# Making one of seven block products of a sequence transform once for two position pairs

## The chip, the cores and the metric

The kernel runs on one core of a Trainium2 chip. The metric is the device time of one launch in microseconds, the median of several runs. TensorE is called PE here, VectorE DVE, ScalarE ACT, GpSimd POOL and SyncE SP, as the profile names them; SP, POOL and, at the very end, ACT issue the DMAs.

## The reference

One input x (2048 positions, width 512) goes through two branches, and a gate mixes them:

```python
g = _sigmoid((x * gate_w).sum(-1, keepdims=True))
# branch A, Fourier mixing: hidden transform, then sequence transform, real part
a = x @ Wd_re.T                      # "bsd,ed->bse"
b = x @ Wd_im.T
A = Ws_re @ a - Ws_im @ b            # "ts,bse->bte", Ws is 2048 x 2048
# branch B, gated MLP with width 1792
h = relu(x @ W_gate) * (x @ W_up)
B = h @ W_down
out = g * A + (1 - g) * B
```

All data are float32.

## The kernel before

**Precision.** A float32 factor is split into a high part (a cast to fp32r, by ACT) and a low part (the rest, a subtraction by DVE). A product takes three matmuls: high by low, low by high, high by high (`PARTS`). In the trace `ch`, `cl` are the two parts of a right side c, `lh`, `ll` or `lb` those of a left side.

**Seven products in place of eight.** Every large product is cut into 2 x 2 blocks and made by the Winograd form of Strassen's method: seven block products, numbered 1 to 7, of sums of blocks. Product 1 is A11 B11, product 2 is A12 B21; block 11 of the result is their sum. Sums, splits and the combination of the results are work for DVE, ACT and the DMA queues while PE multiplies.

**Stages, in order of PE.** Gate and up projections (`Block`, results h to `hd` in HBM), the hidden transforms (`SpectralBlock`, results to `ad`), the last of the gate and up blocks, the down projection (`Down`, two rounds; it stores B to `out` and -B to `zd`), and then four rounds of the sequence transform (`Sequence`), two with the cosine matrix (m = 0) and two with the sine matrix (m = 1). The four are (m, p) = (0, 0), (0, 1), (1, 1), (1, 0), where p is a pair of position blocks of 512.

**One Sequence.** The left side is the transformed hidden data: its two block rows are halves of the 512 hidden columns (256, that is two tiles of 128), its two block columns halves of the 2048 positions to sum over (eight tiles each). The right side holds the matrix for the pair: `r11` to `r22`, each read in four quarters `jj` of two tiles. A product is 4 quarters x 2 left tiles x 2 x 3 = 48 matmuls of 512 columns; a round is seven of them, in the order 1, 3, 5, 7, 6, 2, 4 (the last round begins with 3, and makes its last part in halves of 256 columns). For each quarter SP loads four blocks of r, DVE adds blocks for four of the products, ACT and DVE split seven right sides. `lb` holds split left sides that were stored to HBM during Down and are fetched again for the sine rounds.

**Results.** Products gather in pairs of banks of PSUM (eight in all). The cosine rounds add their four result blocks to `zd` by accumulating DMAs on POOL's queue. The sine rounds add `zd` to the result, also by such a DMA, multiply by the gate (`gg`) on DVE, and add to `out` by a third.

**Who sets the order.** All steps are recorded with a key, the matmul count at which they are wanted. `Plan.due` turns keys into due times, and `Plan.order` sorts the steps of DVE and ACT by them and chooses, engine by engine, the next one that can start by its own costs (0.22667 us for a matmul, a work time for each operation, a line for all DMAs). A step of DVE or ACT may be placed 40 matmuls ahead of its key (`AHEAD`). The order so found is written out: engines work strictly in that order, and a waiting instruction holds up those behind it. Buffers are `UNITS` = 51 units of 128 x 1024 floats.

The low part of a right side is keyed 24 matmuls ahead of its use and the high part 31 (`LO`, `HI`).

Of the kernel before, what the change touches and what calls it, by code (L numbers as in the profile page):

```python
# [89 lines left out]
class Step:  # L90


    def __init__(self, key, engine, name, a, k):
# [10 lines left out]
        self.after, self.start, self.end, self.due = set(), None, None, None  # L104
# [23 lines left out]

class Plan:
# [5 lines left out]

    ISSUE = {"sync": 0.5, "gpsimd": 0.9, "scalar": 0.5}

# [5 lines left out]
    AHEAD = {"vector": 40, "scalar": 40, "sync": 0, "gpsimd": 0}  # L143

    def __init__(self):
        self.ops, self.bufs, self.now, self.steps, self.key = [], [], 0, [], 0

    def op(self, key, f, *a):
        self.ops.append((key, len(self.ops), f, a))
# [14 lines left out]
    def read(self):  # L164
        self.ops.sort(key=lambda o: o[:2])
        for self.key, _, f, a in self.ops:
            f(*a)
        seen, banks = {}, []
# [17 lines left out]
    def due(self):  # L186

        last, n = {}, self.now
        for s in reversed(self.steps):
# [4 lines left out]
            elif s not in last or s.key > 0:  # L194
                end = self.now - (self.SUMS if "accum_op" in s.k else self.STORES)
                last[s] = min(last.get(s, 1e9), min(s.key + self.REST, max(s.key, end)) * self.MATMUL)
            s.due = last[s] - (s.work + self.LANDING if s.name == "dma_start" else 0)
            for x in s.after:
                last[x] = min(last.get(x, 1e9), s.due - self.WAIT - (x.work if x.name != "dma_start" else 0))

    def order(self):
# [5 lines left out]
        free = dict.fromkeys(todo, 0.0)  # L207
        late, line, live, ends = 0.0, 0.0, 0, []
# [5 lines left out]
        while any(todo.values()):  # L214
# [27 lines left out]
            while ends and ends[0] <= t:  # L242
                ends.pop(0)
                live -= 1
# [14 lines left out]
            for b in {r.base for r in (*s.writes, *s.reads) if r.base.kind == "unit"}:  # L259
                left[b] -= 1  # L260
                if not left[b]:
                    ends.append(max(x.end for x in b.uses))
                    ends.sort()
# [28 lines left out]
def kernel(ctx: ExitStack, tc, xP, xG, wf, wgu, wd, cr, ci, wri, gw, out):  # L292

# [52 lines left out]
    class Pair:  # L346
# [10 lines left out]

        def part(self, n, columns):
            return self.banks[n][:, columns]
# [279 lines left out]
    def gate_row(p, key):  # L639

        b = buf("gg")

        def go():
            load(b.all, gd[2 * KD * p:2 * KD * (p + 1)].rearrange("(j i) p -> j (i p)", j=2).partition_broadcast(P))
        op(key, go)
# [80 lines left out]
    class Left:  # L726


        def __init__(self, source, tiles=(4, 4)):
            self.source, self.tiles = source, tiles  # L730
# [17 lines left out]
        def split(self, m, n, key, step):  # L748
            hi, lo = self.t[m, n] = [buf(f"l{x}{m}", [4, HD], F32R) for x in "hl"]
            raw, s = self.side(m, n), slice(self.tiles[n])  # L750
            if m == 4:
# [7 lines left out]
        def prep(self, n, key, step, to=None):  # L759
# [3 lines left out]
            for m in (1, 5, 7, 6, 2, 3, 4):  # L763
# [13 lines left out]
    SUM = {5: 40, 7: 40, 6: 40, 4: 88}  # L777

    class Round:


        ORDER, last = ORDER_Z, False

        def __init__(self, left, counts):
# [11 lines left out]
            for x in self.ORDER:  # L796
                self.seed(x, plan.now)
                self.products(x)
# [8 lines left out]
        def products(self, x):  # L807
            for jj, n in enumerate(self.counts):
                pe(6 * n, self.product, x, jj)

        def product(self, x, jj, tiles=(0, 1), ps=None, columns=slice(None)):
            c = self.c[x, jj]
            ps = ps or self.ps[{1: "A", 3: "E", 5: "B", 7: "D", 6: "B", 2: "A", 4: "G" if self.last else "D"}[x]]
            first, last = x in (1, 3, 5, 7) and not (self.last and x == 3) and jj == 0, jj == len(self.counts) - 1
            if first:
                ps.new()
            for d in tiles:
                ds = slice(d * P, (d + 1) * P)
                for i in range(self.counts[jj]):
                    j = sum(self.counts[:jj]) + i  # L820
                    l = self.left.t[x, j // 4]
                    for n, (a, b) in enumerate(PARTS):
                        mm(ps.part(d, columns), l[a][:, j % 4, ds], c[b][:, i, columns], start=first and i == 0 and n == 0,
# [6 lines left out]
        def evac(self, x, key):  # L830
# [6 lines left out]
            elif x == 6:  # L837
# [5 lines left out]
                if self.last:  # L843
                    op(key + 18, lambda: E().vector.tensor_sub(self.u2.all, o["22"].all, self.n5.all))
                else:
                    op(key + 34, lambda: E().vector.tensor_sub(self.u2.all, self.w.all, self.n5.all))
            elif x == 2:
                self.middle(key)
            elif x == 4:
                self.end(key)  # L850

        def seed(self, x, key):
            pass

        def middle(self, key):
            op(key, lambda: self.both(E().scalar.copy, self.o["11"], self.ps["A"]))
            self.done("11", key + 6)

        def end(self, key):
            def go():  # L860
                for n in range(2):
                    E().vector.scalar_tensor_tensor(self.o["21"][:, n], self.ps["D"][n], -1.0, self.u2[:, n],
                                                    op0=OP.mult, op1=OP.subtract)
            op(key, go)
            self.done("21", key + 6)
# [23 lines left out]
    HALVES = slice(0, N // 2), slice(N // 2, N)  # L889

    class Half:


        def __init__(self, pair, n):
            self.pair, self.n = pair, n

        def part(self, n, columns):
            return self.pair.part(self.n, columns)


    class Sequence(Round):
        HI, LO = 31, 24

        def __init__(self, left, m, p, last=False):
            self.m, self.p, self.last = m, p, last
            if m:
                self.g = gate_row(p, plan.now + 100)
            if last:
                self.ends = Pair("ze")
                self.half = [Half(self.ends, n) for n in range(2)]  # L910

                self.ORDER = (3, 1, *ORDER_Z[2:])
            super().__init__(left, (2, 2, 2, 2))

        def rights(self):
# [5 lines left out]
            for jj in range(4):  # L921
                r = {b: buf(f"r{b}") for b in BLOCKS}
                for b, key in (("11", at[1, jj]), ("22", at[3, jj]), ("12", at[5, jj]), ("21", at[2, jj] - 36)):
                    op(key - 90, lambda r=r, b=b, jj=jj: load(r[b].all, source(b, jj)))
                for x, (o, i) in {5: ("11", "12"), 7: ("12", "22"), 6: ("11", "22"), 4: ("11", "21")}.items():
                    if self.last and x == 4:

                        op(at[6, jj] - 20, lambda r=r, jj=jj: accumulate(r["11"].all, source("21", jj)))
                        continue
                    op(at[x, jj] - SUM[x], lambda r=r, o=o, i=i: combine(r[o].all, r[o].all, r[i].all, 1))  # L930
                if self.last:
                    g = self.gate("21")
                    op(at[4, jj] - SUM[4] + 2, lambda r=r, g=g: E().vector.scalar_tensor_tensor(
                        r["11"].all, r["11"].all, -1.0, g, op0=OP.mult, op1=OP.mult))
                for x in self.ORDER:
                    self.split(x, jj, r[{1: "11", 3: "22", 5: "11", 7: "12", 6: "11", 2: "21", 4: "11"}[x]])

        def products(self, x):  # L940
            if not self.last or x != 4:
                return super().products(x)
            for jj in range(3):
                pe(6, self.product, x, jj, (1,))
            op(plan.now + 2, self.halve)
            for jj in range(4):
                pe(6, self.product, x, jj, (0,))
            for n, h in enumerate(HALVES):
                pe(3, self.product, x, 3, (1,), self.half[n], h)

        def halve(self):
            self.ends.new()
            for n, h in enumerate(HALVES):
                E().scalar.copy(self.half[n].part(1, h), self.ps["G"].part(1, h))
# [3 lines left out]

        def gate(self, b):
            return self.g[:, int(b[1]) - 1].unsqueeze(1).to_broadcast([P, 2, N])  # L960

        def done(self, b, key):
# [4 lines left out]
            if self.last and b == "12":  # L967
                key += 4
            else:
                op(key, lambda: accumulate(o.all, zd[self.place(b)]))  # L970
                key += 42 if self.last else 62
            op(key, lambda: E().vector.tensor_mul(o.all, o.all, self.gate(b)))
            op(key + 6, lambda: accumulate(out[self.place(b)], o.all))

        def middle(self, key):
            if not self.last:
                return super().middle(key)
            z, v = buf("z"), buf("v")
            op(key - 60, lambda: load(z.all, zd[self.place("11")]))
            op(key - 60, lambda: load(v.all, out[self.place("11")]))  # L980

            def go():
                self.both(E().vector.tensor_add, z, self.ps["A"], z)
                E().vector.tensor_mul(z.all, z.all, self.gate("11"))
# [225 lines left out]
```

## Time and profile before

| | us |
|---|---|
| median of three runs | 795.3 |
| lowest and highest | 794.19, 795.4 |
| the profiled execution | 794.13 |
| its span, first to last instruction | 792.4 |

Times in the tables of the profile are us from the start of the span unless marked ns. A group line reads: line, engine, operation, what is written from what, shapes, count, then busy time, mean ns of one, idle time of the engine ahead of them and what ended it. All lines of the kernel are L126, since one helper issues every instruction; so the names of the tiles tell the groups apart. In the 40 slices a digit is the busy share in tenths.

### The profile page before, as it was taken

How to read it: one execution, taken by the hardware profiler on the slowest of the kernel's cores; microseconds unless marked ns; L12 is line 12 of the kernel's file. 1: busy time of each engine (PE TensorE's matmuls, PEld its weight loads, DVE VectorE, ACT ScalarE, POOL GpSimd, SP SyncE). 2: the span in 40 equal slices, each digit the busy share in tenths (PEclk: the TensorE clock that was granted, in tenths of full speed). 3: DMA queues.
4: the chain of work that ended last, by engine and by line, in shares of the span. 5: the costliest groups of instructions: out<-in, count | busy, mean ns of one | idle time of the engine just before them, and what ended most of it. 6: DMA issues, size and time to landing. Idle time of an engine off the chain costs nothing.

```text
span 792.4 us, 9557 instructions
## 1 busy us (share of the span) xinstructions
PE 787.1 (99%) x3470; PEld 651.5 (82%) x3470; DVE 652.1 (82%) x778; ACT 332.6 (42%) x402; POOL 97.0 (12%) x151
## 2 busy tenths in 40 slices
PE   9999999999999999999999999999999999999997
PEld 7888888888888888888888888888888888888886
DVE  7999986868699466999886799997597549966996
ACT  5533221312133234274665668464343335442631
POOL 0101311111112122111121001001000100011001
PEclk9999999999999999999999999999999999999999
DMA  8614553232548599999899989217877994098766
GB/s 320 250 41 164 180 187 146 93 147 94 199 146 267 194 353 398 416 349 342 296 367 415 411 285 371 87 53 223 259 271 282 282 379 132 31 278 253 199 147 133
DMA packets 53888, 187.02 MB, mean 236 GB/s; under 512 B 6225, under 2 KB 6993, under 8 KB 53841
## 3 DMA queue, kind: packets, MB, share of 16 engines
q1 hardware_dynamic: 33680, 113.40, 39.9%
q0 software_dynamic: 20016, 72.89, 28.1%
q8 instruction: 27, 0.44, 0.2%
q14 instruction: 21, 0.16, 0.1%
q10 hardware_dynamic: 144, 0.13, 0.1%
HBM read 117.18 MB, written 69.21 MB: 235 GB/s over the span
## 4 chain that ended last, share of the span: by engine, by line
PE 99%; ACT 0%; DVE 0%; issue 0%
PE z L126 55%; PE c L126 34%; PE a L126 10%; PE warm L126 0%; PE ze L126 0%; ACT z L126 0%; DVE warm L126 0%
## 5 line engine op out<-in xcount | busy, mean ns | idle before, releaser
L126 ACT CAST ch<-r 128x1024 fp32r<-128x1024 f32 x112 | 116.0, 1052 | 132.4 <-DVE r L126 54.0
L126 PE MATMUL z<-cl,lh 128*128 128x512 f32 x420 | 163.4, 389 | 0.0
L126 PE MATMUL z<-ch,lh 128*128 128x512 f32 x420 | 163.4, 389 | 0.0
L126 PE MATMUL z<-ch,ll 128*128 128x512 f32 x420 | 163.4, 389 | 0.0
L126 DVE TENSOR_TENSOR cl<-r,ch 128x1024 fp32r<-128x1024 f32 x112 | 134.3, 1218 | 30.9 <-ACT ch L126 22.3
L126 PE MATMUL z<-ch,lb 128*128 128x512 f32 x444 | 136.8, 389 | 0.0
L126 PEld LDWEIGHTS z<-ch,lb 128*128 128x128 f32 x444 | 83.3, 188 | 17.3
L126 PEld LDWEIGHTS z<-cl,lh 128*128 128x128 f32 x420 | 78.8, 188 | 16.5
L126 PEld LDWEIGHTS z<-ch,lh 128*128 128x128 f32 x420 | 78.8, 188 | 16.3
L126 PEld LDWEIGHTS z<-ch,ll 128*128 128x128 f32 x420 | 78.8, 188 | 16.2
L126 PE MATMUL z<-cl,lb 128*128 128x512 f32 x222 | 86.4, 389 | 0.0
L126 DVE TENSOR_TENSOR r<-r,r 128x1024 f32<-128x1024 f32 x60 | 71.5, 1216 | 2.8 <-DMA r<-ci 2.5
L126 DVE TENSOR_TENSOR cl<-hr,ch 128x1024 fp32r<-128x1024 f32 (+1 forms) x56 | 59.8, 1085 | 13.2 <-ACT ch L126 11.3
L126 ACT CAST ch<-hr 128x1024 fp32r<-128x1024 f32 (+1 forms) x56 | 51.4, 942 | 27.7 <-DMA hr<-hd 13.2
L126 PEld LDWEIGHTS z<-cl,lb 128*128 128x128 f32 x222 | 41.7, 188 | 8.7
L126 ACT ACTIVATE g<-c 128x512 f32<-128x512 f32 x26 | 15.5, 597 | 62.7 <-PE c L126 62.5
L126 PE MATMUL c<-xl,wb0h 128*128 128x512 f32 x104 | 40.5, 389 | 0.0
L126 PE MATMUL c<-xh,wb0l 128*128 128x512 f32 x104 | 40.5, 389 | 0.0
L126 PE MATMUL c<-xh,wb1h 128*128 128x512 f32 x104 | 40.5, 389 | 0.0
L126 PE MATMUL c<-xh,wb0h 128*128 128x512 f32 x104 | 40.5, 389 | 0.0
L126 PE MATMUL c<-xh,wb1l 128*128 128x512 f32 x104 | 40.5, 389 | 0.0
L126 PE MATMUL c<-xl,wb1h 128*128 128x512 f32 x104 | 40.5, 389 | 0.0
(200 smaller groups left out, 1321.4 us busy)
## 6 DMA issues: line engine op xcount, KB each, us to landing
hr<-hd SPq DMA_DIRECT2D x42, 512.0 KB, 7.1
r<-cr SPq DMA_DIRECT2D x32, 512.0 KB, 4.8
r<-ci SPq DMA_DIRECT2D x32, 512.0 KB, 8.9
hd<-hs POOLq DMA_DIRECT2D x28, 512.0 KB, 4.7
lb<-lb SPq DMA_DIRECT2D x28, 512.0 KB, 4.7
ad<-a POOLq DMA_DIRECT2D x16, 512.0 KB, 6.0
l<-ad SPq DMA_DIRECT2D x16, 512.0 KB, 8.8
wr<-wgu SPq DMA_DIRECT2D x14, 512.0 KB, 6.5
```

The costliest lines, as they stand in the source:

```text
L126: getattr(getattr(nc, self.engine), self.name)(*map(ap, self.a), **{k: ap(x) for k, x in self.k.items()})
```

## The change

Product 2, A12 B21, has the same left side for both position pairs of a matrix. It is taken out of the four `Sequence` rounds, which keep six products (order 1, 7, 6, 3, 5, 4), and is made for both pairs at once in a new class `Joint` after the second and after the fourth round. There A12 (256 x 1024) times the two B21 side by side (1024 x 1024) is again cut into 2 x 2 blocks and made by seven products of 12 matmuls, where two direct products had 48 each. The left sides of a Joint are loaded, summed and split on chip and are not stored to `lb`.

Inside a Sequence the result of product 1 is copied, negated, into the banks in which products 6 and 5 go on (`seed`), so fewer sums are left for DVE; in the sine rounds block 12 of `zd` is copied into the banks of product 3 ahead of it, and block 21 is made ready in SBUF and copied into the banks of product 4. Block 11 is finished after the first product. For product 4, three of the four rounds and both Joints sum the block 21 into r by an accumulating DMA; the round (1, 1) loads it and adds on DVE.

The planner reckons with DMA queues of SP and POOL that send packets in turns, lets SP issue up to 40 matmuls ahead, gives POOL 0.5 us more ahead of a transfer, and takes a landing of 2.1 us, 1.5 us later for sums. The diff, cut to its core:

```diff
 class Step:
-            self.work = n * 4 * P / 4096 * 0.157 / 16 * (2 if "accum_op" in k else 1)
+            self.work = n * 4 * P / 4096 * 0.160 / 16 * (2 if "accum_op" in k else 1)
+class Queues:
+    LANDING, LATER = 2.1, 1.5
+    # add(step, start): packets of the queues that have work go in turns; gives step.end
 class Plan:
+    LATE = {"gpsimd": 0.5}
-    AHEAD = {"vector": 40, "scalar": 40, "sync": 0, "gpsimd": 0}
+    AHEAD = {"vector": 40, "scalar": 40, "sync": 40, "gpsimd": 0}
...
-                line = max(line, free[s.engine]) + s.work
-                s.end = line + self.LANDING + (2.0 if "accum_op" in s.k else 0)
+                queues.add(s, free[s.engine] + self.LATE.get(s.engine, 0))
...
     class Sequence(Round):
+        ORDER, NEW, FOUR = (1, 7, 6, 3, 5, 4), (1, 3, 7), "G"
...
+                r = {b: buf(f"r{b}") for b in ("11", "12", "22")}
+                for b, x, t in (("11", 1, 90), ("12", 7, 110), ("22", 7, 105)):
+                    op(at[x, jj] - t, lambda r=r, b=b, jj=jj: load(r[b].all, source(b, jj)))
+                for x, o, a, b, sign in ((7, "12", "12", "22", 1), (6, "11", "11", "12", 1), (5, "12", "11", "22", -1)):
+                    op(at[x, jj] - 40 if x != 5 else at[6, jj] + 10, ...combine...)
+                if self.fourth:
+                    op(at[6, jj] + 14, lambda r=r, jj=jj: accumulate(r["11"].all, source("21", jj)))
+                else:
+                    ...load r21, combine r11 with it...
...
+            if b in ("11", "22"):
+                op(key, lambda: accumulate(o.all, zd[self.place(b)]))
+                key += 50
+            op(key, lambda: E().vector.tensor_mul(o.all, o.all, g))
+            op(key + 6, lambda: accumulate(out[self.place(b)], o.all))
...
+            if x == 1:
+                op(key, seed)                     # banks B <- -A, by ACT
+                op(key + 1, lambda: both(copy, o["11"], a))
+                self.done("11", key + 6)
+            elif x == 6:
+                op(key, lambda: both(minus, u, b))
+                op(key + 1, lambda: [E().vector.tensor_sub(u[:, n], u[:, n], d[n]) for n in range(2)])
+                if self.m:
+                    op(key + 6, lambda: accumulate(u.all, zd[self.place("21")]))
+                op(key + 50, seed4)               # banks G <- u, by ACT
+            elif x == 5:
+                o["12"] = w
+                op(key, lambda: both(copy, w, b))
+                op(key + 1, lambda: both(E().vector.tensor_add, o["22"], d, w))
+                self.done("22", key + 6)
+                op(key + 7, lambda: both(E().vector.tensor_add, w, e, w))
+                self.done("12", key + 12)
+            elif x == 4:
+                op(key, lambda: both(copy, o["21"], g))
+                self.done("21", key + 6)
+    class Joint:
+        ORDER = (1, 7, 6, 5, 2, 3, 4)
+        def __init__(self, m, last=False):
+            self.m, self.last, self.base, self.lead = m, last, plan.now, 130 if last else 85
...
+            for x in self.ORDER:
+                if last and x == 4:
+                    for h in range(2):
+                        pe(6, self.halves, h)     # bank H0, then H1, 256 columns each
+                else:
+                    for jj in range(2):
+                        pe(6, self.product, x, jj)
+                    self.evac(x, plan.now)
...
+            for x, o, *sums in ((1, "11"), (7, "12", ("12", "12", "22", 1)), (6, "11", ("11", "11", "12", 1)),
+                                (5, "12", ("12", "11", "22", -1)), (2, "21"), (3, "22"), (4, "11")):
+                for a, b, c, sign in sums:
+                    op(at[x] - 6, ...combine...)  # at[x]: place of the product less self.lead
+                if x == 4:
+                    op(at[6] + 6, lambda: accumulate(r["11"].all, source("21")))
...
+            if x == 1:
+                op(key, seed)                     # bank X <- -A, by ACT
+            elif x == 6:
+                op(key, lambda: e.scalar.copy(s, bank("X")))
+                op(key + 1, lambda: e.vector.tensor_add(y, bank("D"), s))
+                if last:
+                    op(key + 2, seed4)            # banks H0, H1 <- v - g y
+            elif x == 5:
+                op(key, lambda: e.vector.tensor_add(o[1][:, 1], bank("B"), y))
+                op(key + 2, done, 1, 1)
...
-        Sequence(lefts[m], m, p, n == 3)
+        Sequence(lefts[m], m, p, n != 2)
+        if n % 2:
+            Joint(m, m == 1)
```

More of the change, by code (lines that the diff above doesn't have):

```diff
@@ L103, in __init__ @@
             self.reads += self.writes
-        self.after, self.start, self.end, self.due = set(), None, None, None
+        self.after, self.start, self.end, self.due, self.rest = set(), None, None, None, None
         n = writes[0].size() if self.writes else 0
@@ L195, in due @@
                 end = self.now - (self.SUMS if "accum_op" in s.k else self.STORES)
[L196 removed]
+                last[s] = min(last.get(s, 1e9), min(s.key + s.rest, max(s.key, end)) * self.MATMUL)
             s.due = last[s] - (s.work + self.LANDING if s.name == "dma_start" else 0)
@@ L199, in due, with last @@
                 last[x] = min(last.get(x, 1e9), s.due - self.WAIT - (x.work if x.name != "dma_start" else 0))
+    @staticmethod
+    def last(b):
+        return max(x.end for x in b.uses)
     def order(self):
@@ L241, in order @@
             now = t
-            while ends and ends[0] <= t:
+            while over and ends[0] <= t:
+                over.remove(min(over, key=Plan.last))
                 ends.pop(0)
@@ L261, in order @@
                 if not left[b]:
-                    ends.append(max(x.end for x in b.uses))
-                    ends.sort()
+                    over.append(b)
+            ends = sorted(map(Plan.last, over))
             done.append(s)
@@ L796, in __init__ @@
             for x in self.ORDER:
-                self.seed(x, plan.now)
-                self.products(x)
+                for jj, n in enumerate(counts):
+                    pe(6 * n, self.product, x, jj)
                 self.evac(x, plan.now)
@@ L887, in done, with __init__, fill @@
             op(key + 8, lambda: store(zd[t, :, es], n.all))
[L889 to L898, printed above, removed]
     class Sequence(Round):
+        ORDER, NEW, FOUR = (1, 7, 6, 3, 5, 4), (1, 3, 7), "G"
         HI, LO = 31, 24
-        def __init__(self, left, m, p, last=False):
-            self.m, self.p, self.last = m, p, last
+        def __init__(self, left, m, p, fourth):
+            self.m, self.p, self.fourth = m, p, fourth
             if m:
[L907 to L912, printed above, removed]
-            super().__init__(left, (2, 2, 2, 2))
+                self.NEW = (1, 7)
+                self.g = gate_row((2 * p, 2 * p + 1), plan.now + 100)
+                z = buf("z")
+                op(plan.now + 80, lambda: load(z.all, zd[self.place("12")]))
+                op(plan.now + 130, self.fill, z)
+            super().__init__(left, (2, 2, 2, 2))
+        def fill(self, z):
+            e = self.ps["E"]
+            e.new()
+            for n in range(2):
+                E().scalar.copy(e[n], z[:, n])
         def rights(self):
@@ L931, in rights @@
[L931 to L934, printed above, removed]
-                for x in self.ORDER:
[L936 to L949, printed above, removed]
@@ L973, in done @@
             op(key + 6, lambda: accumulate(out[self.place(b)], o.all))
[L975 to L984, printed above, removed]
-                E().vector.tensor_add(v.all, v.all, z.all)
-                load(out[self.place("11")], v.all)
-            op(key + 4, go)
```

280 lines of the change are left out of this document (184 added, 96 removed).

## The prediction

> **What bounds the kernel now.** I read the page's head and its 40 slices first, then the chain of waits in order of time.
>
> ```profile
> span 792.4 us, 9557 instructions
> ...
> PE 787.1 (99%) x3470; PEld 651.5 (82%) x3470; DVE 652.1 (82%) x778; ACT 332.6 (42%) x402; POOL 97.0 (12%) x151
> ...
> PE   9999999999999999999999999999999999999997
> ...
> PEclk9999999999999999999999999999999999999999
> DMA  8614553232548599999899989217877994098766
> ```
>
> ```profile
> 1.06 3.43 PE warm L126 x8
> ...
> 350.18 436.56 PE z L126 x1926
> 786.74 1.44 PE ze L126 x12
> ...
> 788.20 0.37 ACT z L126
> ```
>
> After the warm-up's end at 4.49 us PE has no gap, at a full granted clock, and the chain is PE to its last matmul. So the time is the number of matmuls, the 4.5 us ahead of them and the 4.2 us behind (792.4 - 788.2). One 512-column matmul is 436.56 / 1926 = 0.2267 us; the twelve 256-column ones took 1.44 us with the drain of the last, about half each. No wait ends late anywhere on PE. What can change the time is therefore the count of matmuls, or an operand that PE would have to wait for. The windows show how near the others are: the first row is the densest stretch of the Down stage, the next four are one Sequence each (PE, PEld, DVE, ACT, POOL, clock, DMA share, GB/s).
>
> ```profile
> 317.00:396.00 79.00, 79.00 (x350) 65.44 (x349) 75.45 (x90) 43.16 (x52) 11.78 (x19) 1.00 0.95 351
> 483.00:559.00 76.00, 76.00 (x337) 62.91 (x336) 67.66 (x65) 38.50 (x42) 3.64 (x5) 1.00 0.52 168
> 559.00:636.00 77.00, 77.00 (x341) 63.79 (x340) 55.92 (x52) 30.57 (x33) 3.36 (x4) 1.00 0.85 278
> 636.00:712.00 76.00, 76.00 (x337) 62.91 (x336) 59.94 (x56) 33.31 (x38) 5.16 (x6) 1.00 0.61 198
> 712.00:788.00 76.00, 76.00 (x342) 63.14 (x340) 66.43 (x62) 28.45 (x32) 8.54 (x10) 1.00 0.73 188
> ```
>
> In the Sequence stage DVE is busy 67.66 + 55.92 + 59.94 + 66.43 = 250.0 of 305 us, 82%. The first row says that 75.45 of 79 us of DVE (96%) and a DMA share of 0.95 are still compatible with PE at 79.00 of 79.00.
>
> **The matmuls.** Before, each of four Sequences has seven products of 48 matmuls, 1344 in all. After, each has six, 1152, and each of two Joint blocks has seven products of 12, 84 together: 1320. That is 24 fewer, on the path in full: 24 x 0.2267 = **5.44 us**. The built program agrees: 3470 matmuls with twelve half-wide before, 3452 with 24 half-wide after. The twelve more halves have the price of six wholes by the row of ze; bounds -0.1 to +0.1 us, taken as 0.
>
> **DVE in the stage.** In the built program its 1024-element operations go from 340 to 343 and its 512-element ones from 351 to 379. Up to four of the 1024-element ones that go (low parts of product 2's left side) lie before or at the edge of this stage, so the stage gets up to 7 and 28 more. What one costs is read from starts in its timeline.
>
> ```profile
> 753.60 4.70 DVE L126 TENSOR_TENSOR cl<-r,ch 128x1024 fp32r<-128x1024 f32 x4
> 758.22 1.22 DVE L126 SCALAR_TENSOR_TENSOR r<-r,gg 128x1024 f32<-128x1024 f32 x1
> ```
>
> ```profile
> 359.55 0.68 DVE L126 TENSOR_TENSOR hs<-h,h 128x512 f32<-128x512 f32 x1
> 360.15 0.69 DVE L126 TENSOR_TENSOR hs<-hs,h 128x512 f32<-128x512 f32 x1
> ```
>
> A 1024 takes (758.22 - 753.60) / 4 = 1.155 us, a 512 takes 360.15 - 359.55 = 0.60 us. So 7 x 1.155 + 28 x 0.60 = 24.9 us more: 274.9 of 305 - 5.4 = 299.6 us, 92%. On average it fits; all of it lies beside PE and I count it as 0. The cover is thinnest at the end, where the last Joint's operands (keyed up to 130 matmuls early) stand among those of the last Sequence. Between the low part cl of product 4, second quarter, in the third Sequence and the last one of product 4 in the fourth, DVE has 59 operations of 1024 and 13 of 512: 59 x 1.155 + 13 x 0.60 = 75.9 us, while PE has 312 matmuls, 70.7 us. So DVE must bring a lead of 5.2 us and may not idle beyond the rest. Low parts are keyed 24 matmuls ahead and may start 40 earlier, so its lead is between 24 x 0.2267 - 1.2 = 4.2 us and 64 x 0.2267 - 1.2 = 13.3 us.
>
> **The new wait in that stretch.** The last Sequence's block 11 is now finished after its first product, and its gate multiplication stands in DVE's order behind a sum by DMA: ACT copies (four of 512, two of them the new bank seed), POOL issues the sum, it lands, DVE multiplies. Behind that multiplication are queued 28 more 1024s and nine 512s up to the last cl of product 4; POOL's next three sums of r wait behind the store of its result.
>
> ```profile
> L126 ACT COPY z<-z 128x512 f32<-128x512 f32 x8 | 4.6, 588 | 11.5 <-PE z L126 9.8 <-DMA z<-zd 1.7
> L126 ACT CAST ch<-r 128x1024 fp32r<-128x1024 f32 x109 | 113.1, 1053 | 132.4 <-DVE r L126 54.0 <-PE z L126 49.1 <-DMA r<-ci 15.1
> ```
>
> ```profile
> r<-cr SPq DMA_DIRECT2D x32, 512.0 KB, 4.8
> r<-ci SPq DMA_DIRECT2D x32, 512.0 KB, 8.9
> ...
> z<-zd POOLq DMA_DIRECT2D x5, 512.0 KB, 8.2
> ...
> r<-ci POOLq DMA_DIRECT2D x4, 512.0 KB, 9.0
> ```
>
> ```profile
> q1 hardware_dynamic: 33680, 113.40, 39.9%
> q0 software_dynamic: 20016, 72.89, 28.1%
> ```
>
> From product 1's end the sum is there after 4 x 0.588 + 8.2 (issue included) = 10.6, with the wake-ups and POOL's start some 11.4 us. The multiplication and what is queued behind it is 29 x 1.155 + 9 x 0.60 = 38.9 us, so the last cl is ready at 50.3 us; PE wants it 228 matmuls after product 1's end, at 51.7 us. It is in time by **1.4 us**. A wait here costs nothing to a DVE that is behind anyway, since the landing has a fixed place against PE, which is why I take 0 and not the ends: 0 below (PE has no idle to win back), and above what the rivals give.
>
> **The DMA queues.** POOL's sums go from 23 to 40 of 512 KB (12 instead of 4 into r, 4 into jr, 24 instead of 19 into u, z, w, zd and out); SP's loads of the stage grow by about 4.5 blocks net. q0's rate is 0.281 x 792.4 / 72.89 = 3.05 us per MB: 17 x 0.524 x 3.05 = 27 us if a sum counts its bytes once, 54 if twice, plus 4.5 x 0.524 x 0.399 x 792.4 / 113.40 = 7 us. On a mean share of 0.68 x 305 = 207 us that is 241 to 268 of 299.6: 0.80 to 0.90, under the 0.95 that PE bore. The planner now reckons with two queues in turns and lets SP issue 40 matmuls (9 us) earlier; that moves orders in all stages, with no instruction more. PE has nothing to gain there; at worst it loses a first wait of some 4 us (8.9 against 4.8 below). I take 0, by the row 317:396.
>
> **Short products.** In a Joint a product is 12 matmuls, 2.72 us. The bank for product 6 is seeded by ACT while product 7 runs: 0.588, or 1.64 behind one cast, both under 2.72; behind three casts 3.75, a loss of 1.0 in each Joint. Product 3 goes on in product 5's bank once DVE has read it (0.6 plus at most one 1.155 before it), also inside 2.72. Taken as 0, bound +2.1 us together.
>
> **The end.** As before, the last half bank goes by a copy on ACT and ACT's own DMA:
>
> ```profile
> out<-z SPq DMA_DIRECT2D x1, 256.0 KB, 2.7
> ...
> out<-z ACTq DMA_DIRECT2D x1, 128.0 KB, 2.3
> ```
>
> Product 3's block needs three DVE operations (1.8 us) and 2.7 us to land, 4.5 us after product 3; the last half lands 2.72 + 0.4 + 2.3 = 5.4 after it. So the same tail, 0, between -0.2 and +0.5.
>
> **Sum.** 794.13 (the profiled execution) - 5.44 = 788.7. The median of the runs, 795.3, stands 1.2 above that execution, so the forecast is 795.3 - 5.4 = **789.9 us**.
>
> **Rivals.**
> *Late sums.* The gate's sum lands late. In this trace the transfers that touch z took between 4.0 and 13.5 us to land:
>
> ```profile
> DMA to landing us min/median/max: 4.0/7.9/13.5
> ```
>
> At 13.5 it is 5.3 us later than 8.2, and 5.3 - 1.4 = 3.9 us reach PE: 789.9 + 3.9 = 793.8. For it: r<-ci took 8.9 where r<-cr took 4.8, and ci's loads run beside sums. Against: the median of that row is 7.9. The Trainium skill ("DMA: Bandwidth & Descriptors", section on queues, rings and completion order) has each DMA engine go round-robin between the queues that have work. The pair 4.8 and 8.9 agrees with it; by that rule a sum that met an idle SP queue at 8.2 would take 16.4 beside a busy one, PE would lose 6.8 us, and the sum would be 796.7.
>
> *DVE becomes the bound in the last Sequence and Joint (slower).* Besides a late sum DVE goes on idling as now: 76 - 66.43 = 9.6 of the last 76 us, 12.6%, hence 38.9 x 0.126 / 0.874 = 5.6 us over the queue behind the gate. The waits of the stage say what for:
>
> ```profile
> DVE cl L126 <- ACT ch L126: 22.3, 12, 5.0
> DVE z L126 <- PE z L126: 14.0, 4, 4.2
> ```
>
> With the sum at 13.5 PE then waits 5.6 + 5.3 - 1.4 = 9.5 us: 799.4. It decides for slower once lateness and idling together pass 1.4 + 5.4 + 1.6 = 8.4 us. For it: 75.9 us of work in 70.7. Against: much of the idling is that of a DVE ahead of its operands, and goes when it has a backlog; the Down stage ran at 96%. One consequence more: the program's first eight matmuls took 3.43 / 8 = 0.43 us each, against 0.2267 later. The Trainium skill ("TensorE: Matmul & The Clock Gate", Part 1) explains this with a clock that is halved after about 3.4 us without work and given back after as long; by it a single wait of 9.5 us would cost eight slow matmuls, 1.6 us, on top: 801.0. No row shows a later idle PE.
>
> *A wait of the middle size*, one operand 4.1 us late (8.9 - 4.8) at any of the new DMA orders: 794.0.
>
> **How the numbers follow.** A measurement can tell about 0.2%, 1.6 us, from no change. The forecast with at most a small wait (up to 793.7): 0.60. Late sums or one late operand (793.7 to 796.9): 0.13. DVE as the bound: 0.27. The low end is the lowest run, 794.19, less 5.44 and the tail's 0.2: 788.6. The high end is the slower rival's 799.4; above it I leave about 0.13, below the low end 0.03. The forecast's own range is 788.6 to 792.
>
> **What would show it.** Right: 3452 matmuls, PE groups without idle, DVE about 90% busy behind 490 us, and a chain that is PE up to the last half bank. The step on DVE is wrong if PE's idle stands ahead of z<-cl or a Joint's matmul and names DVE; the step on sums, if DVE's wait at z<-z,gg or POOL's landing is over 10 us; the short products, if PE waits for jX or jB. The whole is wrong if PE's busy time falls by other than 5.4 us or the span by less than 3.8.

## The result, and the profile after

| | before | after |
|---|---|---|
| median of the runs, us | 795.3 (5 runs) | 790.69 (5 runs) |
| lowest and highest | 794.19, 795.59 | 789.66, 792.18 |
| the profiled execution | 794.13 | 789.66 |
| its span | 792.4 | 787.6 |

The ratio is 0.9947, 95% interval 0.9932 to 0.9961: 4.6 us faster by the medians, 4.5 between the profiled executions. A second set of five runs of the same kernel (e5 below) had a median of 789.84, with a ratio of 0.9939 (0.9927 to 0.9952).

The head of the page after:

```profile
span 787.6 us, 9681 instructions
PE 782.4 (99%) x3452; PEld 647.9 (82%) x3452; DVE 672.1 (85%) x808; ACT 364.5 (46%) x457; POOL 109.6 (14%) x164
```

The chain of waits after, in order of time (start, us, what):

```profile
350.63 263.84 PE z L126 x1164
614.48 2.72 PE jA L126 x12
...
633.51 130.80 PE z L126 x576
...
780.63 2.88 PE jH L126 x24
...
783.60 0.37 ACT jo L126
```

It is PE from end to end, as before. PE's stage began at 350.18 and ended at 788.18 before (438.00 us); now it begins at 350.63 and ends at 783.52 (432.89). That is 5.11 less, where 24 matmuls make 5.44. The rest is in two rows: 576 matmuls at 0.2267 are 130.56 us and took 130.80, and the 24 half-wide ones took 2.88, that is 0.120 each, against 0.113 for half a whole one (0.08 us for the twelve more). The stage began 0.45 us later, the stretch behind the last matmul is 0.1 shorter, and what lies outside the span grew from 1.7 to 2.1 us: -5.11 + 0.45 - 0.12 + 0.33 = -4.45.

The windows after, two Sequences without and two with a Joint (PE, PEld, DVE, ACT, POOL, clock, DMA share, GB/s):

```profile
483.00:548.00 65.00, 65.00 (x289) 53.84 (x288) 56.70 (x54) 35.91 (x42) 7.04 (x9) 1.00 0.75 225
548.00:633.00 85.00, 85.00 (x377) 70.41 (x376) 74.05 (x74) 50.73 (x62) 9.77 (x12) 1.00 0.82 238
633.00:698.00 65.00, 65.00 (x289) 53.83 (x288) 56.33 (x52) 31.50 (x37) 5.66 (x7) 1.00 1.01 349
698.00:783.00 85.00, 85.00 (x386) 70.56 (x385) 82.26 (x86) 47.36 (x62) 12.86 (x15) 1.00 0.82 194
```

DVE is busy 269.3 of 300 us, 90%, but 82.26 of 85 (97%) in the last row, where the densest row of this stage before had 67.66 of 76 (89%). The 0.24 us that PE lost lie there. PE's timeline after, then DVE's (start, duration, in brackets the idle time ahead and what ended it):

```profile
760.97 0.61 PE L126 MATMUL z<-ch,lb 128*128 128x512 f32 x2
761.51 0.50 PE L126 MATMUL z<-cl,lb 128*128 128x512 f32 x1
761.85 0.63 PE L126 MATMUL z<-ch,lb 128*128 128x512 f32 x2
```

```profile
720.95 1.22 DVE L126 TENSOR_TENSOR z<-z,gg 128x1024 f32<-128x1024 f32 x1
...
730.74 0.69 DVE L126 TENSOR_TENSOR u<-u,z 128x512 f32<-128x512 f32 x1 [0.62 <-ACT u L126]
732.73 1.22 DVE L126 TENSOR_TENSOR jr<-jr,jr 128x1024 f32<-128x1024 f32 x1 [1.30 <-DMA jr<-ci]
...
760.24 1.21 DVE L126 TENSOR_TENSOR cl<-r,ch 128x1024 fp32r<-128x1024 f32 x1
```

The low part that starts at 760.24 is the last cl of product 4; PE wanted it at 761.43 and it was there at 761.45. The gate multiplication of block 11 began at 720.95 with no idle time ahead of it, so the sum by DMA was not late. Between the two DVE idled 1.9 us, once for ACT and once for a load of a Joint's right side.

### The profile page after: what moved, and what is told of

Same layout as the page of the kernel before. It is cut to its first block, busy times and chain, and to the rows that moved or that the text cites. A ratio compares the mean times of both kernels' runs of the same rounds, so it can differ in the third digit from the quotient of the medians.

```text
span 787.6 us, 9681 instructions
## 1 busy us (share of the span) xinstructions
PE 782.4 (99%) x3452; PEld 647.9 (82%) x3452; DVE 672.1 (85%) x808; ACT 364.5 (46%) x457; POOL 109.6 (14%) x164
## 4 chain that ended last, share of the span: by engine, by line
PE 99%; ACT 0%; issue 0%; DVE 0%; ACTq 0%
PE z L126 50%; PE c L126 34%; PE a L126 10%; PE jB L126 1%; PE jA L126 1%; PE jX L126 1%; PE jD L126 1%; PE warm L126 0%; PE jH L126 0%; PE jG L126 0%; ACT jo L126 0%; DVE warm L126 0%; ACTq L126 0%
## 5 line engine op out<-in xcount | busy, mean ns | idle before, releaser
L126 PE MATMUL z<-ch,ll 128*128 128x512 f32 x388 | 151.0, 389 | 0.0
L126 PE MATMUL z<-ch,lh 128*128 128x512 f32 x388 | 150.9, 389 | 0.0
L126 PE MATMUL z<-cl,lh 128*128 128x512 f32 x388 | 150.9, 389 | 0.0
L126 ACT CAST ch<-r 128x1024 fp32r<-128x1024 f32 x96 | 99.5, 1052 | 67.2 <-DVE r L126 34.8
L126 DVE TENSOR_TENSOR cl<-r,ch 128x1024 fp32r<-128x1024 f32 x96 | 115.8, 1220 | 13.7 <-ACT ch L126 6.3
L126 PE MATMUL z<-ch,lb 128*128 128x512 f32 x384 | 118.3, 389 | 0.0
L126 PEld LDWEIGHTS z<-ch,lb 128*128 128x128 f32 x384 | 72.1, 188 | 14.9
L126 PE MATMUL z<-cl,lb 128*128 128x512 f32 x192 | 74.8, 390 | 0.0
L126 POOL DMA_DIRECT2D hd<-h x28 | 17.8, 639 | 178.9 <-DVE h L126 178.9
L126 ACT COPY t<-c 128x512 f32<-128x512 f32 x26 | 15.1, 587 | 55.2 <-PE c L126 55.1
L126 PE MATMUL c<-xl,wb0h 128*128 128x512 f32 x104 | 40.5, 389 | 0.0
L126 PE MATMUL c<-xh,wb1h 128*128 128x512 f32 x104 | 40.5, 389 | 0.0
L126 PE MATMUL c<-xh,wb0l 128*128 128x512 f32 x104 | 40.5, 389 | 0.0
L126 PE MATMUL c<-xh,wb0h 128*128 128x512 f32 x104 | 40.5, 389 | 0.0
L126 PE MATMUL c<-xh,wb1l 128*128 128x512 f32 x104 | 40.5, 389 | 0.0
## 6 DMA issues: line engine op xcount, KB each, us to landing
lb<-lb SPq DMA_DIRECT2D x24, 512.0 KB, 12.1
```

Source lines behind the costliest of these rows:

```text
L126: getattr(getattr(nc, self.engine), self.name)(*map(ap, self.a), **{k: ap(x) for k, x in self.k.items()})
```

## The experiments

Each run stands beside its own runs of the kernel before. "Gain" is the difference of the two medians.

| run | edit of the changed kernel | us | before | gain | ratio, 95% |
|---|---|---|---|---|---|
| e1 | 4 more low parts on DVE, last Sequence | 794.31 | 794.82 | 0.5 | 0.9995 (0.9986 to 1.0004) |
| e2 | the same, first Sequence | 792.87 | 794.82 | 2.0 | 0.9980 (0.9970 to 0.9990) |
| e3 | 4 fewer sums on DVE, last Sequence | 789.23 | 794.82 | 5.6 | 0.9927 (0.9913 to 0.9940) |
| e4 | planner of before | 792.41 | 794.82 | 2.4 | 0.9968 (0.9957 to 0.9980) |
| e5 | none | 789.84 | 795.08 | 5.2 | 0.9939 (0.9927 to 0.9952) |
| e6 | kernel before with the new planner | 794.59 | 795.08 | 0.5 | 0.9997 (0.9988 to 1.0006) |
| e7 | 4 sums from DVE to POOL's DMA, last Sequence | 794.41 | 795.08 | 0.7 | 0.9993 (0.9984 to 1.0001) |
| e8 | the same, first and last Sequence | 800.85 | 795.08 | -5.8 | 1.0073 (1.0061 to 1.0086) |
| e9 | product 4's parts 16 matmuls earlier, last Sequence | 791.97 | 795.12 | 3.2 | 0.9956 (0.9943 to 0.9968) |
| e10 | the same, 24 | 791.12 | 795.12 | 4.0 | 0.9953 (0.9940 to 0.9966) |
| e11 | last Joint's left sides 380 matmuls earlier | 795.46 | 794.90 | -0.6 | 1.0015 (0.9997 to 1.0033) |
| e12 | e11, and last results summed by DMA | 798.16 | 794.90 | -3.3 | 1.0045 (1.0031 to 1.0059) |

### Is it DVE's load in the last Sequence? (e1, e2, e3)

e1 and e2 compute four low parts of product 7 twice, 4.6 us of DVE; e3 takes four sums out.

```diff
 # e1 (e2: m == 0)
             op(self.at[x, jj] - self.LO, lambda: E().vector.tensor_sub(lo[:, s], raw[:, s], f32(hi[:, s])))
+            if getattr(self, 'm', 0) == 1 and self.p == 0 and x == 7:
+                op(self.at[x, jj] - self.LO, lambda: E().vector.tensor_sub(lo[:, s], raw[:, s], f32(hi[:, s])))
 # e3
+                    if x == 5 and self.m and not self.p:
+                        continue
                     op(at[x, jj] - 40 if x != 5 else at[6, jj] + 10, ...combine...)
```

> The changed kernel, with the four low parts of product 7 in the last Sequence computed twice on DVE (four more operations of 1.14 us, 4.6 us, the same values). Theory 'DVE has no time left there': the last Sequence's low parts were ready just as PE wanted them, so what is added comes out in the time: 790.7 + 4.6 = 795.3, at least 793 if other work moves behind them; PE waits for DVE ahead of z<-cl in the last Sequence. Rival 'count of matmuls alone': DVE still has a reserve, 790.7 within 1.

> The changed kernel, with the four low parts of product 7 in the first Sequence computed twice on DVE (4.6 us more, the same values). Both theories say 790.7 within 1, since DVE has idle time in the first Sequence; a rise of over 2 us would say that DVE's average load and not the last stretch is what counts.

> The changed kernel without the four DVE sums for the right side of product 5 in the last Sequence (4.6 us of DVE less; product 5 there takes another right side). Theory 'DVE has no time left there': the last wait of PE goes, 0.3 to 1.2 us faster, 789.5 to 790.4, and the runs lie closer together than 789.7 to 792.2. Rival 'count alone': 790.7 and the same spread.

In e3 the last Sequence's matmuls take just their own time. The row of its chain and its last window:

```profile
633.92 130.56 PE z L126 x576
```

```profile
698.00:783.00 85.00, 85.00 (x386) 70.77 (x385) 79.18 (x82) 48.20 (x62) 12.94 (x15) 1.00 0.82 196
```

With DVE at 79.18 in place of 82.26 us the 0.24 us are gone (130.56), and the gain is 5.6 us: what the count of matmuls gives. The median, 789.23, lies even under the 789.5 to 790.4 that I expected. Its five runs lie between 788.32 and 789.58; of the ten runs of the changed kernel, eight lie above that. Since e3 leaves out four sums that the result needs, it shows a price and is no kernel to use. In e1, PE's waits behind 481 us were these (total, times, longest), and the clock falls in the window that holds the end:

```profile
PE jH L126 <- DVE jcl L126: 1.8, 1, 1.8
PE jH L126 <- DVE jt L126: 1.5, 1, 1.5
```

```profile
780.00:790.00 10.00, 6.05 (x34) 4.89 (x32) 8.15 (x12) 2.47 (x6) 0.00 (x0) 0.89 0.22 74
```

So 4.6 us more of DVE cost 3.6 to 4.5 us of time, as 794.31 is set against the two medians of the changed kernel. The waits don't stand where I expected them, ahead of a cl of the last Sequence: its matmuls and the third's together took their own time, 130.56 us. They stand ahead of the last Joint's product 4, so the added work was handed on to the end. In the profiled execution (795.52, the slowest of the eleven) the stage was 4.1 us longer than in the profile after: 3.3 are the two waits, and the slower clock of the last matmuls is part of the rest. Another 1.7 us were lost before the stage, which began at 352.36. So from the last Sequence to the end a microsecond of DVE is nearly a microsecond of time.

In e2 I was wrong: the first Sequence isn't free either (2.2 to 3.0 us by the same medians). There are two waits of 1.7 us together in it, with DVE at 59.13 us (56.70 above):

```profile
PE z L126 <- DVE cl L126: 1.7, 2, 1.3
```

```profile
483.00:548.00 65.00, 63.10 (x275) 50.93 (x274) 59.13 (x56) 36.30 (x42) 7.05 (x9) 1.00 0.71 222
```

The average of 56.70 in 65 us hides that DVE is full in the first half of this Sequence: in the window 483:515 of the profile after it is busy 31.97 of 32 us. Ahead of it, at the end of Down (440 to 483), it is busy 39.65 of 43 us, so it can do little of the work ahead of time. DVE is thus short of time in two places, and e1 and e3 alone don't single out the last.

### Is it the planner? (e4, e6)

```diff
 # e4, its core: planner of before in the changed kernel (e6: new planner in the kernel before)
-    AHEAD = {"vector": 40, "scalar": 40, "sync": 40, "gpsimd": 0}
+    AHEAD = {"vector": 40, "scalar": 40, "sync": 0, "gpsimd": 0}
...
-                queues.add(s, free[s.engine] + self.LATE.get(s.engine, 0))
+                line = max(line, free[s.engine]) + s.work
+                s.end = line + self.LANDING + (2.0 if "accum_op" in s.k else 0)
```

> The changed kernel with the planner of before (one line for all DMAs, SP not ahead of its keys, 0.157 a packet, sums 2.0 us later). Theory 'the planner is needed': with 17 more sums by DMA the one line puts loads and sums too late, PE waits for operands, 793 to 800. Rival 'the saving is the matmuls alone': 790.7 within 1.

> The kernel before with the new planner alone (queues in turns, SP 40 matmuls ahead), products as before. Theory 'count of matmuls': PE had no wait to win back, so 794.8 within 0.5. Rival 'the planner brings part of the gain': over 1 us faster, under 793.8.

e4 takes back the reckoning of the DMAs and the earlier start of SP; how the planner keeps book of the buffers stays new. In e6 there is no difference to measure (interval 0.9988 to 1.0006), so the planner brings nothing of its own beyond 1 us. In e4 the changed kernel keeps only 2.4 us, and 792.41 lies in neither of the ranges that I gave: the planner of before places the new work worse. e4's longer wait of PE behind 481 us:

```profile
PE z L126 <- DVE cl L126: 0.7, 1, 0.7
...
```

It is the same last cl of product 4; the other wait is of 0.2 us. Besides, from PE's last matmul to the end of the span it took 5.9 us in e4, 4.1 after.

### The same kernel again (e5)

> The changed kernel as it is, beside the others of this call. Theory 'no time left on DVE in the last Sequence': a median of 790 to 791.5 with runs spread over 2 us or more, and a profile with a wait of PE of 0.2 to 2 us for DVE ahead of the last low part of product 4 in the last Sequence. Rival 'count alone': runs within 1.3 us, as before, and no wait of PE there.

The median, 789.84, lies just under the 790 to 791.5 that I expected; the spread, 2.3 us, and the wait are as expected. Here the wait at the same cl is long enough for the chain to leave PE. The chain of e5 from 633 us on:

```profile
633.77 84.12 PE z L126 x372
717.90 15.55 DMA jr<-ci
...
735.30 1.14 DVE jr L126
...
761.07 1.15 DVE cl L126
762.26 2.79 PE z L126 x11
```

Read backwards: PE's matmul at 762.26 was released by the cl of 761.07; from there the chain is DVE at work back to 735.30, and DVE's backlog began with a sum that had waited for a load of the Joint's right side, jr, which took 15.55 us. The view of waits gives 0.4 us for this one. So the late operand is an SP load that stands beside POOL's sums, and not the sum of the gate. The chains of e8, e9 and e11 hold such a load of jr too (16.28, 17.27 and 11.81 us).

### Does moving DVE's sums to POOL's DMA help? (e7, e8)

```diff
                 for x, o, a, b, sign in ((7, "12", "12", "22", 1), ...):
+                    if x == 7 and self.m and not self.p:      # e8: not self.p
+                        op(at[x, jj] - 72, lambda r=r, jj=jj: accumulate(r["12"].all, source("22", jj)))
+                        continue
```

> The changed kernel, with the four sums of product 7's right side in the last Sequence made by accumulating DMAs on POOL's queue in place of DVE (4.6 us of DVE less, four sums by DMA more, same result). Theory 'no time left on DVE': the last wait of PE goes and the full 5.44 us are saved, 789.0 to 789.7, runs close together. Rival 'sums by DMA late': the block 12 comes too late for product 7 and PE waits there, 791 to 794.

> As the run with the last Sequence's sums of product 7 by DMA, and the same in the first Sequence (eight sums by DMA more). If DVE's shortage is in the last Sequence alone, no faster than that run, 789.0 to 789.7; if the first Sequence also costs in some runs, up to 0.5 us faster; if its sums are late beside the many loads at its start, over 791 with PE waiting ahead of product 7 of the first Sequence.

DVE has four operations less in e7, yet nearly the whole gain is lost; 794.41 is above both ranges that I gave. PE's waits in e7, both in product 4 of the last Sequence and not in product 7, where the rival had them:

```profile
PE z L126 <- DVE cl L126: 1.5, 1, 1.5
PE z L126 <- ACT z L126: 1.2, 1, 1.2
```

The DMA view of the stretch 690 to 783, after and then e7 (queue: packets, MB, share; issues: count, KB each, median us to landing):

```profile
q0 software_dynamic: 2448, 8.91, 53.5%
...
jr<-ci SPq DMA_DIRECT2D x8, 512.0 KB, 12.5
```

```profile
q0 software_dynamic: 3024, 11.01, 64.1%
...
jr<-ci SPq DMA_DIRECT2D x8, 512.0 KB, 15.9
```

POOL's queue q0 takes 64.1% in place of 53.5%, and the loads of jr beside it land after 15.9 us at the median in place of 12.5. DVE saves four sums and waits for data instead (between 698 and 783 us 4.2 us for r, 1.7 for jr and 2.0 for a sum of zd). e8 shows what happens where the first Sequence is loaded as well:

```profile
PE z L126 <- DVE cl L126: 3.9, 3, 1.5
PE z L126 <- ACT ch L126: 2.8, 1, 2.8
PE z L126 <- ACT z L126: 1.3, 1, 1.3
```

That is 8.0 us of waits, and the clock of PE fell behind the first two. The first two are in product 7 of the first Sequence, and the chain goes back from PE's next wait, at 511.41, to a sum by POOL into r, issued at 480.79, that took 16.48 us. e8's PE timeline and the clock in a window over it:

```profile
498.39 0.50 PE L126 MATMUL z<-ch,ll 128*128 128x512 f32 x1 [2.79 <-ACT ch L126]
499.78 0.57 PE L126 MATMUL z<-cl,lh 128*128 128x512 f32 x1 [0.89 <-DVE cl L126]
500.14 0.63 PE L126 MATMUL z<-ch,lh 128*128 128x512 f32 x1
...
503.53 0.39 PE L126 MATMUL z<-cl,lh 128*128 128x512 f32 x1
```

```profile
500.00:503.50 3.50, 3.50 (x9) 2.72 (x9) 3.46 (x4) 1.90 (x2) 0.00 (x0) 0.51 1.06 287
```

Eight matmuls start between 500.14 and 503.53, 0.424 us each, 1.6 us more than at full clock.

### Would another order do? (e9, e10)

```diff
-            op(self.at[x, jj] - self.HI, ...)      # high part, ACT
-            op(self.at[x, jj] - self.LO, ...)      # low part, DVE
+            early = 16 if x == 4 and getattr(self, "m", 0) and not self.p else 0   # e10: 24
+            op(self.at[x, jj] - self.HI - early, ...)
+            op(self.at[x, jj] - self.LO - early, ...)
```

> The changed kernel, with the high and low parts of product 4 in the last Sequence keyed 16 matmuls earlier; no work is taken away, and DVE's order then has the last low part ahead of block 22's sums. Theory 'it is the order of a full DVE in the last Sequence': the wait of PE ahead of that low part goes, 789.0 to 789.7 beside a kernel before of 794.8 to 795.1, with runs closer together. Rival 'DVE's load alone': the wait moves to the Joint's low parts of product 4 (1.5 us in hand there), 789.8 to 791.

> As the run with 16 matmuls, with 24: the Joint's own parts then come later in DVE's order. By the order theory 789.0 to 789.7 as with 16; by the load theory the Joint waits by up to 2 us, 790 to 792.

In e9 the wait at the last cl is gone and another is there, 1.7 us for ACT: the bank seed of product 4. Neither theory had it there, and 791.97 is above both ranges. ACT's timeline in e9 ahead of it:

```profile
750.74 1.05 ACT L126 CAST jch<-jr 128x1024 fp32r<-128x1024 f32 x1 [2.73 <-DVE jr L126]
751.70 1.05 ACT L126 CAST ch<-r 128x1024 fp32r<-128x1024 f32 x1
752.65 1.98 ACT L126 CAST jch<-jr 128x1024 fp32r<-128x1024 f32 x2
754.54 1.10 ACT L126 COPY z<-u 128x512 f32<-128x512 f32 x2
```

The seed (the copy into z) stands behind four casts, the first of which waited 2.73 us for a sum of DVE; in the changed kernel it was copied at 750.9. In e10 PE waits nowhere behind 481 us, and still nothing is won: its last matmul ends at 783.38, but the span lasts 5.3 us beyond it. e10's DVE timeline at the end:

```profile
783.31 1.29 DVE L126 TENSOR_TENSOR jo<-jo,jv 128x512 f32<-128x512 f32 x2
```

DVE ends at 784.60 instead of 783.67, and SP's store of that result is issued and lands later: the wait has moved behind PE's end. Order doesn't make room where DVE has none.

### Is there room a round earlier? (e11, e12)

```diff
-            self.lefts(self.base - 60, 10)
+            self.lefts(self.base - (440 if last else 60), 10)
 # e12 besides, in Joint's done:
+                    if (p, n) != (1, 0):
+                        accumulate(out[2 * p, :, n], f)
+                        return
```

> The changed kernel, with the last Joint's left side (4 sums and 7 low parts of 512, 6.6 us of DVE) keyed 440 in place of 60 matmuls ahead, so that DVE makes it in the third Sequence, where it has 8.7 us idle; same result. Theory 'DVE is full from the last Sequence to the end': with 6.6 us less there PE's wait and the late results at the end go, 789.0 to 789.7, about e3's 789.2 with all work done. Rival 'units or loads': ten units held 85 us longer put loads of r late, and PE waits in the third or last Sequence, 791 to 795.

> As the run with the left side a round earlier, and two of the Joint's three result blocks are added to the output by accumulating DMAs in place of a DVE addition (1.2 us of DVE less at the very end). If DVE still sets the end: 0.3 to 0.8 us faster than the run with the left side alone. If the sums by DMA land after the last half bank: up to 3 us slower.

e11's waits of PE behind 481 us, then DVE's between 698 and 783 us, and the window of that stretch:

```profile
PE z L126 <- DVE cl L126: 3.5, 5, 1.5
```

```profile
DVE jr L126 <- DMA jr<-ci: 3.9, 2, 2.7
DVE r L126 <- DMA r<-ci: 2.5, 1, 2.5
```

```profile
698.00:783.00 85.00, 81.46 (x353) 65.55 (x353) 77.66 (x73) 46.26 (x56) 12.84 (x15) 1.00 0.82 190
```

DVE is less busy there than in the changed kernel (77.66 against 82.26), as some of its work was moved out, and PE waits 3.5 us: the rest comes later because its data do. SP issued the first two loads of jr at 715.11 in place of 709.71 and the last two at 728.06 in place of 722.22; that the buffers held longer are the reason, as the rival had it, is likely but not shown. The median, 795.46, is just above the rival's range. In e12 the span ends 6.5 us behind PE's last matmul (789.4 of 795.9). In e11 that stretch is 3.7 us (788.9 of 792.6), so most of the 2.7 us between the two medians is there. Late landings don't explain it: POOL's two sums of results were issued at 782.80 and 785.41 and took 5.1 us, and SP's closing waits, which stand behind the last transfers, ended at 792.54. What ended last in the trace was POOL's own closing DRAIN, from 785.39 to 794.80. An earlier load of the last Joint's right sides, which e5's chain would ask for, was not tried; nothing that was tried with all its work done beat the changed kernel.

## Why the prediction was right

**The matmuls: right.** 24 fewer, 3452, and PE's stage 5.11 us shorter, where the count alone makes 5.44. e3 shows the full sum as a gain (5.6 us), and e6 that the planner adds none of it.

**DVE at no cost: right on average, too low by 0.2 to 0.4 us in place.** 92% was forecast for the stage, 90% measured. The place was right to the instruction: the last cl of product 4 in the last Sequence. The term that was mis-sized is the margin of 1.4 us there. The first part came out as forecast (11.2 us from product 1's end at 709.7 to the gate multiplication, 11.4 forecast), though partly by luck: the sum had landed at 720.1, and DVE came to the multiplication at 720.95, when the work ahead of it was done. But from that multiplication's start to the last cl's end it took 761.45 - 720.95 = 40.5 us, where 38.9 was the work alone: DVE idled 1.9 us of it, and the prediction had put its idling at nought in the forecast and at 5.6 in the rival. So the operand that was to be early by 1.4 us was just late, with a loss of 0.24 us after and of 0.4 in e5, and e1 shows how hard the edge is. That the idling came out nearer to nought than to 5.6 is luck as well: nothing in the prediction gave its size.

**The new wait (the gate's sum): right as no wait, wrong as the thing to fear.** The gate's sum was issued at 710.60 and landed 9.5 us later, still ahead of DVE. What came late were loads on SP's queue, jr with 15.55 us in e5's chain. Loads of cr in the stage took 8.9 us to land, against the 4.8 shown before. Neither the added sums nor SP's earlier start makes this alone: the same row reads 6.0 in e4 (the added sums without the earlier start) and 5.4 in e6 (the earlier start without the added sums). Nor is it the number of sums: e8, with eight more, has 6.0 again. The row after:

```profile
r<-cr SPq DMA_DIRECT2D x24, 512.0 KB, 8.9
```

The loads of lb went from 4.7 to 12.1, and with them it is the changed work: 12.7 in e4, 5.9 in e6. The Trainium skill ("DMA: Bandwidth & Descriptors", section on queues, rings and completion order) has each engine go in turns between queues with work. By an estimate from that, a transfer beside a busy queue takes up to twice its time; the step of jr from 12.5 to 15.9 in e7, with four sums more, goes that way, but the runs don't bear out the factor. The pair of 4.8 and 8.9 for cr and ci, in which the prediction saw it, is 5.4 and 6.9 in e6 with the same transfers, so it hangs on the order of issue too. The prediction put the risk on the sum; it was loads that grew longer, and most of them were still in time.

**DMA share: right.** 0.75, 0.82, 1.01 and 0.82 make 254 of 300 us, 0.85; 0.80 to 0.90 was forecast. Queue q0 went from 28.1% of 792.4 to 34.0% of 787.6 us:

```profile
q0 software_dynamic: 21888, 79.70, 34.0%
```

That is 45 us more, between the 27 and 54 of the two readings.

**Short products: right.** Every product of a Joint but the last takes 2.72 us in the chain, 12 x 0.2267: no wait. **The end: right for this kernel.** 4.1 us behind PE against 4.2; it isn't a constant, though: 5.9 in e4 and 5.3 in e10, where DVE was late.

**The planner at nought: right in e6, but not the whole of it.** By itself it changes nothing that can be measured; for the changed work it is worth about 1.7 to 2.6 us (e4 against the two medians of the changed kernel).

**The slower rival.** Its mechanism is real and near: e1 lost 3.6 to 4.5 us to 4.6 more of DVE, and e8 shows the price of the clock that it named, eight matmuls and 1.6 us. It didn't decide because DVE's idling (1.9 us) stayed under the point that was worked out for it. The late-sum rival didn't occur after. More sums on POOL's queue brought such waits, though not for the gate's sum: DVE waited 4.2 us for r in e7, and a sum into r took 16.48 us in e8.

**What is not settled.** The 0.45 us by which the stage began later is lost in the first 6 us: the loads there are issued at the same times to 0.01 us, but in PE's timeline the first matmul on data starts at 4.64 instead of 4.44 us, and the first four take 1.43 instead of 1.19. The two profiles with the planner of before start the stage sooner than all with the new one, by 0.3 to 1.3 us and by 2.2 in e1, but e6 shows no loss by it in its median, and two profiles are too few. Some of the spread of the changed kernel's runs may come from there and not from DVE.

## What to carry to other kernels

Where PE has no gap, count its instructions first: what is taken off PE comes back in full only as long as every helper's queue keeps its lead, and that is read where the lead is smallest, not from the stage's average (56.70 of 65 us was already too much in e2's place). When two helpers are full, moving work from one to the other, or ahead in the order, only moves the wait (e7, e9, e10, e11); of what was tried only leaving work out helped (e3). Follow the chain of a disturbed run of the same kernel: it names a transfer that eats into the margin, which the undisturbed run hides. Whether an earlier transfer gives the margin back is open here.

## What the runs showed of the hardware

The clock of PE fell to half without a single long pause. In e1 two waits, of 1.5 and 1.8 us in the rows above, with some 1 us of matmuls between them, brought 0.89 in that window: the half-wide matmuls from 787.85 us on took 0.21 us in place of 0.12. e1's PE timeline:

```profile
783.59 0.36 PE L126 MATMUL jH<-jch,jt 128*128 128x256 f32 x1 [1.47 <-DVE jt L126]
...
786.44 0.38 PE L126 MATMUL jH<-jcl,jt 128*128 128x256 f32 x1 [1.79 <-DVE jcl L126]
...
788.05 0.41 PE L126 MATMUL jH<-jcl,jt 128*128 128x256 f32 x1
788.26 0.63 PE L126 MATMUL jH<-jch,jt 128*128 128x256 f32 x2
```

In e8 waits of 2.79 and 0.89 us brought 0.51 for 500.00 to 503.50. The Trainium skill ("TensorE: Matmul & The Clock Gate", Part 1) gives half the clock after at least one idle window of about 3.4 us. The length of the slow stretch, 3.4 us in e8, agrees with such a window; that PE must be idle without a break for as long does not, since the longest wait was 2.79 us. Waits that lay further apart, 1.7 us in two in e2 and 3.5 us in five in e11, left the clock at 1.00 in their windows. How much idle time in which stretch is enough, these runs don't show.

POOL's closing DRAIN, which begins at its last issue of a DMA, took between 8.1 (e8) and 12.7 us (e4) in the profiles of this case, 9.4 in e12. Elsewhere it was over before the last transfers; in e12, where that issue came late, it set the end.
